# One kernel, its instruction order replaced: local and block-summary attention with an FFN behind it, on one Trainium2 core

## The chip, the cores and the metric

The kernel runs on one core of a Trainium2 chip. A core has five engines with an instruction queue each: TensorE (PE, with PEld for its weight loads), VectorE (DVE), ScalarE (ACT), GpSimd (POOL) and SyncE (SP). In this kernel SP does nothing but issue DMA transfers. Engines run their own queues in order and wait for one another by semaphores. The time is the device time of one execution in microseconds (us); the number that counts is the median of several executions.

## The reference: what is computed

The inputs are q, k and v, 4 batches, 8 heads, 768 positions, 64 elements, and the weights of a layer-norm (LN) and of an FFN.

```python
k_sum = k.reshape(B, H, nb, 32, D).max(axis=3)      # 24 blocks of 32 keys
v_sum = v.reshape(B, H, nb, 32, D).mean(axis=3)
mask_l = np.abs(pos[:, None] - pos[None, :]) < 16   # local window
scores_s = scale * einsum('bhsd,bhnd->bhsn', q, k_sum) + np.log(32)
a = softmax(concat([where(mask_l, scale * q @ k.T, -1e9), scores_s]))
x = (a @ concat([v, v_sum])).transpose(0, 2, 1, 3).reshape(B, S, 512)
xn = (x - mu) / sqrt(var + 1e-6) * g_ln
out = x + maximum(xn @ w_ch1, 0) @ w_ch2            # 512 -> 2048 -> 512
```

## The kernel before

The 3072 rows of x (4 x 768) are worked on in 24 tiles of 128 rows. For a tile, the queries of one head meet only a band of keys around them and the 24 block maxima, so the scores are narrow. Tiles 0 to 5, the first batch ("early", in two halves of four heads each, t = 0 to 11: `early_k`, `early_qk`, `softmax`, `early_transp`, `early_pv`) are worked on in float32 while the FFN weights are fetched and prepared. Tiles 6 to 23 ("late": `load_q`, `load_k`, `load_v`, `heads`, `late_softmax`, `values`, `late_out`) are worked on in split float16: a value is carried as a float16 and a rest, and products are summed from several matmuls. Weights arrive as `raw` (512 KB transfers) and are merged to `m` on DVE (`merge_w`); `gram` multiplies them with themselves, the `scales` for each group of rows come from the gram sums, a diagonal matrix `diag` from the scales, and PE then makes `low`, the scaled low-order part of the weights (`split_w`).

The FFN takes two tiles at a time, a group. The step `norm` runs LN over a tile: mean and variance (`mv`) on DVE, the root `rs` on POOL, x16 on DVE, and a DMA transposition of x16 (128x8x128, half a group) to `xt`. FFN stages `g1(s)` make hidden blocks h0, h1, ... (48 or fewer matmuls `h<-xt,w_u` of 256 columns); `g2` and, from group 3 on, `g2_wide` multiply them with the second weights, in banks a or acc_a, acc_s, acc_o; `parts_of` splits the hidden values with tiles called wide, on ACT and DVE. The sums come back as `uv`, are added to x on POOL (`x<-x,uv`) and on DVE, and go out. `batch` makes for each batch block maxima and sums (`kmax`, `vsum`), from loads into `bst`, of which there is one buffer.

What sets the order: none of these operations is issued where its line stands. Class `Plan` records every call of an engine as an entry of `self.ops` (a `unit` joins several matmuls into one), and `issue` (line 159) then issues the entries in the sequence that the constant `ORDER` gives, a compressed list of numbers at lines 58 on. Hence every instruction has line L159 in the trace. The one list orders all five engines: an engine runs its own entries in the sequence that they have in the list, and waits are added where an entry needs another engine's result or a buffer that is not free. DMA issues share 8 semaphores in turn, so that a ninth transfer waits for the first to have landed. Pools, tile sizes and the number of buffers are set by the constants ahead of `ORDER`. `warm` stands for 36 matmuls of the identity matrix `ident` with itself, whose result is not used; `gain` spreads the LN weights over 128 partitions by a matmul with ones.

Of the kernel before, what the change touches and what calls it, by code (L numbers as in the profile page):

```python
# [55 lines left out]
AT = {4: 16, 5: 19, 6: 23, 7: 24, 8: 26, 9: 30, 10: 33, 11: 37, 12: 41, 13: 46, 14: 51, 15: 54, 16: 60, 17: 63, 18: 67, 19: 71, 20: 76, 21: 79, 22: 84, 23: 87}  # L56

ORDER = (
    "c-l3X2Y6Lg_QltE^pKcPrPlxnEkG!t8#*H3U;zcB7You92WCbEDFcEaDxfG*1Qk#;G-*mzno92wK@y~w(BYjuzx(|EKR#Ywx%ZsC*Is+=b#7_hu`5<p"
    "2d#uMtccFreaod{x^LO}Kg_-9E9s2gwrnb???bi2ABARyuh~_b7#bbEWS(DgtERH-G=J||luGG_l~X~jXO%0~NDu71ov{wA+t%&$mn@`n<`n$P!Ifsc"  # L60
    "oKr|<9o^7yy2Wy5buF?a#j1?<SrzTEIGwVh%B}kDM_)yMvUe37u*<ww(>$xD8cMTuHb6yn)^4yub+_C%(qC5DZSm!_jq6G&Ne^wG<xq@1Cze_|N!+XL"
    "8GemXqRXpC$#1n)aL#U7KCl=XdOuu3tL!<|Cbqp+ScSD+kJx;Bp2+uGqApvUyX`xKUJMsecTKjZ-C5r!wAOF*GnM5Ih3o4ZV!L6<nq*CN+V)#_K4rS1"
    "ey$By4V&#MSTy&{unBIV@8%9!5i1kQ^85W*n@vX5+!bG2kGM0w3W%3bs@rWxe03$c4gQ=B4(0I^c|949bNhVj(86$Yx6_*Fpf5x8Np69!<Z@VcS5vv&"
    "bz;dN^4GOc&F!3=J!V_nLm#%BnrmH^&Fx{`g;vES+a7xXY<GjuCI6^?v)bCKJXXj3>f3-%4PwY?$*!0^qNN&Pzk}K%T>ogKo~zlnl-+Q7{c2E}tEcU{"
    "Tj3j6dm>t@RLfF9R}6H<`gJm{-(e|w=yN!)K7O_xp_*;r!`tpHf5yscrEBg#=iY~Qikjqbm0`_FqHmz8cFZ=qRx0ZcsFEF%sM<*%@3w(+Mf+HH6>Gh0"
    "u9~>JzAEeHajX1D8}IU3KD(x5nDh(##8{$hV(Z)~?|63|tXqN7Qr%M#PcEwMa$BnX>{k0GuCgzoOq;28Zn3@YkHE=6Hb(DRF`cmSYN#f*MY-YZ9gEg4"
    "+G>qe+D<4<Md1H(z2h(1eivi8Ky#-(R1RC|T9eHk7}?0SDTUp}_-U%>;^?_5TH%kAM=6&|&7RV?*4Ul3tE%K5(^rc11(f3ExG%Z#Ghdiq`q5>x4K~u="
    "RWq%#*7{!2)>2<;lAoZ~s!d;hrCvnxhh3rmZ`uQ!%5L%6XwQUpg!jPf7!|S|%5N7~znO~LS$^B(JGi#i&~~bUt#a*rrlxD0KcPgsuCIJAozf*+qA7ld"
    "3aNr+!tY0@?|y&C)mI(6VBKML61s9lk5id+ze{ndVjE$>9XNAY$E*_T4AiUcWxI}we5nsXJzW>z=3Q!*XkWNQy0W76WyN}S&WaO3H~DZ_IZ=#;egil*"
    ")sO0o9>nP?j2!Mp``?s|qCB+Ez1e(M!rItA?b3F8)!x%%>h0IL!*p}-`%L!=pNdk4WZMi*e`<`LQxq#Zed_vi|8`YYVVmS?=`*XPH~e%r%ujS9{CXE<"  # L70
    "jcuAsq?WN(8b!JZORHNU+p4B?RwKU?ZL4DwU9wsc(OT8hUK{G)bxEvO3-0}@>x#EBusCE7)S6Z6npdiy>Ka-d6!N0W@?WX3{y>wrTLa7HirZ=JvUaFm"
    "NmTWaE}}^BI%==mx2Us$cwJ>jC(l|_vT3GUK9}p~deg(>U0OIz^%Zo-F-x&DrP$;8mA^Gmumb4vHmip+#-V~4uqsObaEroSLx=n?KDT>RE#3FwuI^)B"
    ")1B}sZk_ef9A5{7cldTL%@=h~(Qj$tMAtx@?Kmo4z&^HXzByM^baTS}-8a6n3szm_3pwxmx|t|QJ$Ks<`s{8bTHrLwP4J2Ch=0Ldw=}<)ie6Cx>e3>#"
    "k)1QOF&wrQp%?smwX|h)#~gLHb}mMfL9UI<w8cI(RLZ{aO+!U(i8XaU`I|OS?^;jx%%S4$jG=hUf=W6}o{gPpbGWMZs+rpy26dMnK5M2TI%1ufI8k)W"
    "d3ADI!qv4xc|l`axKXI0ZT9KJz17cmlYBmxKZwJ%x5D<kJKzrxZAxfoxU%xQ2ihLKppNcNcpu*$P<7Tj=lc3Bii2ZMxi!88x>+amjepvOG|lS!Xcw<p"
    "=;6OD3yxK=bQQFVaCN2HE0=SAsh+fTYU`%c4W-b(T*?HiG-?&2Emnr_2dk(5PIc4~C3;;QwAa^gWw~~<vdP;4e+=#<X%l_k))u%fO!&^srCatncmAN="
    "zOEanPprOGceCtwKL~ElclGThy#S|v^GR;L&9M&dHF`6f*6WZTtkP~S)2O?4syAIaQ4=)Ey7;lG<UH4;pzQCdp*4iP+tfAC8#mM{Fk{NNN^0x#tB0=H"
    "vuMXmTY$!7*fLwF|Ej!oL8s%H;*Pod9CP&x`f8bdp}?O6ZlN|D@1XB&lHF05X;lkUCuoa;&QC*O9@ugH!{V9TLFVt+Kb2Fr6l3G<6HP-$@+$%Lzo4SF"
    "UmfubJ?O}bXxxk1uj@WdU9Bcc_`PnT?c1z+#F;EbQL3RD&B69R8f%*^pF3u|tQ+?&w;xcYA!vJ&8*C@-4K>m*o$%$=!%eo~R)^Xx)AJh0T>8>x!N}D("
    "qsOSrli-mUOiexT-LzP3EddpHo)}9~nLN5{ziFy1qTgnNMh`7PZ`<?fo^{b;6t6X}In-0;KSOPz^eK3bv$uKIiaF3qsc7g$`-b`Po^JTjdY^yOEd$M+"  # L80
    "z!ZvA&(QR6YrCteeuk?KGaK6`TwFVlc%Sa+g)^9E{WY8^HwFAo>z*&*s)crk(OG*_GkAT~7SgFX;g-`J`;Ms*72#Xp(Xyykc~uQ93OB$-o@3ILCfkak"
    "W#J5JPzHZ_)2fAf_<z|Y++vnxfaVNp_K{832%JMFT?fn7RPwSC?4}*EuW=(sEO+S3a4aer7b@Ym*mf#4&30S+(9Q5o+i3OB_*&px4&*v$4KpFjhM|`W"
    "a5WcjDTlZsy9R;mO75zo-T2-0?DHdzrz6#CM^s1A+-vs09Sx6HEgKTL7mm^6IKES^pwF~#K=~pQsy_WPM91+db+y#p4^L)BRL8Yt;G_$a@h$rcb?jts"
    "QIjXM+={sr?tK$yTbjGl-SfVqp0kR28Yh}yYlx&gl|5)J^poWZ<%B<dsa){Bt#1)|_pLs}H}11*;P;OGo1V!F@~xSCtGK@#`rl7u=#XC`8WBy`jkK@a"
    "6#pAjxF#_t(vdNAWEGY32VAUz9=mJ>(U1qY=X5+vIh@e~OCY0n^){}n8pzFLHV=m{Neb4z%KBT$X{g#!tCo7wRrgQgQ=92UoY+t;qu-uEm-e~s_}T@o"
    "v459U({Mr8tv|0<tt@_O9@;!b>DCwiZgT_tDD`7%p76bGvg)~mJ_=V=l>HnPPu6Wb;0oTq;>P;6%-P+XGm>CflqwP59(r<=HPaFeu*23{=a?K<bj<JL"
    "yFzZ8UkLhfOvqT)7_HweY-P~e-e5PC{(DL#ao|_z-4lKkeX;`Qw4Lsp%JlwFUsLNP%!ExAa)H0}C}AEtz615F45F8aY9}2VB8~vbCOF~w_Jpg7S6OR;"
    "E3HMP-lrQcz~?CSf{#~WU0*8m66c&KT+;-bN2m9<ajr1;{)|ctv}av&8)!dK%??cXhSVq6r(VQoZ?O6<6P^7p3_NRTR?rP$>Sj|3YIzX-OvAUo$Fx39"
    "r3$)di6j>;=qM5V!b}LN-c~=*M}wJmXE>qlM#C0pmaVZ(c+3J^7gX^UZgGaDfXJI@!2r529X5=`pOZISn?`1*L1h+f?1$Fhp&G~0&aJ4&96D}2r=8w#"
    "Fu3!yUekD=%6|Pck+?_V7yE&7UG=x8$)OsPco=oL4LU1q75W~-OgU_waI`aQrJkVscU#~JejxUHRDUX!Oa{Np)|am9OT5SM-MPWFIcJiyOp-%>Jcz8Z"  # L90
    "z088mc7yd>(UpN`nrSQTbM<AP54h(T_(Tgw!yZ9hC&0u{RgG+>Yd%wQ2j{<Za=A^8eNc%paA7`KwxNzC(7=wc>0#hG=--ZTd^J;M4qmn@=yxQpd(856"
    "^zQ5UtvT>&Fn&FsO5@Nwa(8=tzz9w|$I<UN?p{ls7e~~6DiMF6Hh71%c*`^PPus)pv($$Z+bT{Rb-7{{Q+FLK&!L~G<9*aG6($uV?w(}23S4`j#hdI;"
    ">w$W`jb5FEv3pVZMRZCdI6DIbdN6^4{0pObi{WfM>$HT)|6(eS<nH2}d+IWaAEk1=IqSWT>P-RTaZIJ!WHkb%7!6BCvCi*QXcP*3*80Gs85+&5CG|2f"
    "*3(3y9ti@&nWx#9Oz|4exxJkYQd>?_(JHPkoJ~upJQM8`@>xzVOh>b$abOATSdDqN!XH&T^t%Xm&cL;HVC{wAe+ykb4EA|p$K#sn6Wj@AP*dIaFY8&>"
    "?*}4Z*ej7I8^@{Ua8?<@6-{tbWl`1Acz{Ltliv6r@p~ur*LbR&gu{4)S^Npz+K&h}vExcxi#m;hxen%}!q`-hd&ws0B`Pux7A-*2b5q|QRA)9Pgf5(?"
    ")}W&!nUF<5>=lqPCe+*N$#icDwo5osC(~I|*)g4dTTA|qj0U3~Df%9bZ_aP|(Vk3ez-e<6{V)h+2qJ8RFY@rF2Dp3xudm`9=E9*v<QJkwl{Jo-mlMxI"
    "ChS78xQ_zu1HDG5Yj%a)AR7%QvuqkCx^eX0Jot7AcT*Qfo`Bo=1g#BLtHJkqsqKF7?xuYD3tu#dy-G06qZK^siAJHy!mh4dS(^WORDs<%wbFwr>I|n-"
    "R1>Y4&NU@L|0rD&kL#_jCtz2yD#P%xxY*edOea`8`V~XW2Vwdm6k;#&Hc~9>eWrQjxCQ_5G4)@GdL_Ba%+6171kb^pMj$=_H$0u$u@z2az<`6yxWk-H"
    "Cc)xjU|tO5_mj!X>>N1D1l^C|zKa}wM~nVNCv`(50_{sA!!amP6?QwW7PbKf&w$+*S+g7+_>lfdpf_rv3umZDPX&%68+WaNaW5!%!u2bi^%`y}l^kx{"
    "WNXg14K+m1QoY^wD)VlUUbDdUeqg~I|4^^;%copBnCfN2gWQfhHw&ipVH{NgYQGA^OOsD3-<-!y90%#XsPSMj53bE1<Ce^f@?_K*#V*E)axW7r3Op+k"  # L100
    "Yh85bwtY<v>*5(s;S>(qI}u-8i4N(8m--Kr`T*U$gjsmn4&Zz~0?|bJIe6|@0Y&?WX;J|sN3-f%U^ya!UKSJlF1(osezBZLiqPc)B7OV@HM?$sZl7X}"
    "gH|Ns^5bA^OB{E3c+`YnD&fQ`z`QlQCMkHbcn6iQ2iAcvD6gXMF9W<c)0<cLCh(p4U`?7mNyh}JbSKAnlxGn$sw%5@)=M^1fo~s9Hx1Da3!XpK;ADOe"
    "9gd;rojTC($>e^J&jEfV;d?BV&7^~(nIKgaJYPH#na3URyXA=DMfzw1x;GItcTwTBRQL>2aU}Q0!L%$YwVN37@hQ-%jWG8nceG|c^dhfd?gUR>b5Rcm"
    "hWp{b{m7H0(@d8WDE<Sk_`x3Hmf8^6ACY;RP8W}d@#Q0PupCO!9aULGM@~Z{c2b9pRG|sIKTM_2=a<1UA6{<)I((Df>ID1mL^x6`g5P;+nn`Xatq?gU"
    "pn6B?%UqG3h>FbjJ8-U;f^*4jbikn&e}aEb-fgEw1tT>I>i+k$-MkUDW>bDvx{KoHQ~|IGa>>beS0if#D_^t!e+`~I=ZV}KLxdp(d!)m$Vv)~*+8&KO"
    "p^j$fLQIAzRg64IE*iNflSy@hDIQ#Vm*3t0{rfxi4DS5<bCAz@IOovIum#Vcy#*)M;IDzO@hLmM{tpwyAg="
# [996 lines left out]
```

## Time and profile before

| what | us |
|---|---|
| median of 3 executions | 596.71 |
| lowest, highest | 595.60, 597.96 |
| the profiled execution | 598.19 |
| its span, first to last instruction | 596.4 |
| busy: PE, PEld | 576.2, 466.1 |
| busy: DVE, ACT, POOL | 488.9, 413.9, 128.8 |

The profiled execution is one of its own, 1.5 us above the median. A row of the trace is one instruction or several equal ones in a row; in brackets it has the idle time of its engine ahead of it, and what ended it. Matmuls are pipelined: a row's length is the sum as modelled, and equal ones overlap.

### The profile page before, as it was taken

To read this page: it belongs to the slowest core of one execution; us is meant where nothing else is said; L and a number is where in the kernel's file an instruction comes from. 1 tells how busy PE (TensorE), PEld (TensorE's weight loads), DVE (VectorE), ACT (ScalarE), POOL (GpSimd) and SP (SyncE) were. 2 spreads that over 40 slices of the span, in tenths; PEclk is the share of its full clock that TensorE was granted. 3 is DMA by queue.
4 is the path that set the end of the run, shared out by engine and by line. 5 is a ranking of instruction groups with operands and counts; after the bars stand their busy time and mean duration, and the time that the engine had idled before them with its cause. 6 is when DMAs were issued, how large, how long until landed. Compare 5 with 4: busy or idle time off the path is not lost.

```text
span 596.4 us, 16606 instructions
## 1 busy us (share of the span) xinstructions
PE 576.2 (97%) x6440; PEld 466.1 (78%) x6440; DVE 488.9 (82%) x1290; ACT 413.9 (69%) x1043; POOL 128.8 (22%) x213
## 2 busy tenths in 40 slices
...
GB/s 286 242 276 282 257 253 245 224 98 114 129 156 118 138 156 123 148 95 147 163 124 121 129 65 109 93 108 118 81 118 94 89 70 75 81 71 41 36 2 35
DMA packets 108484, 79.19 MB, mean 133 GB/s; under 512 B 68733, under 2 KB 94973, under 8 KB 108406
## 3 DMA queue, kind: packets, MB, share of 16 engines
...
## 4 chain that ended last, share of the span: by engine, by line
PE 41%; DVE 12%; ACT 6%; DMA 4%; issue 3%; SPq 1%; POOL 0%; ACTq 0%; DVEq 0%; POOLq 0%
PE h L159 20%; PE acc_a L159 8%; PE acc_s L159 6%; PE acc_o L159 5%; DVE h_x L159 3%; DVE wide L159 3%; DMA bst<-in_ks 2%; ACT p L159 2%; ACT h_x L159 2%; PE o L159 1%; DVE x L159 1%; SPq L159 1%; PE s L159 1%; DVE p L159 1%; ACT wide L159 1%
## 5 line engine op out<-in xcount | busy, mean ns | idle before, releaser
L159 PE MATMUL h<-xt,w_u 128*128 128x256 f16 x2304 | 265.7, 273 | 3.5 <-DMA xt<-x 1.1
L159 PEld LDWEIGHTS <-w_u 128*128 128x128 f16 x2304 | 224.1, 98 | 34.6 <-issue 6.6
L159 PEld LDWEIGHTS <-h_x 128*128 128x128 f16 x1752 | 170.7, 98 | 45.5 <-issue 0.6
L159 DVE TENSOR_TENSOR h_x<-wide,h_x 128x896 f16<-128x896 f32 x72 | 80.6, 1128 | 23.5 <-ACT h_x L159 23.0
L159 ACT CAST h_x<-wide 128x896 f16<-128x896 f32 x72 | 66.5, 934 | 47.1 <-DVE wide L159 46.9
L159 DVE TENSOR_TENSOR wide<-wide 128x128 f32<-128x128 f32 (+1 forms) x224 | 78.8, 363 | 19.8 <-ACT wide L159 17.5
L159 POOL TENSOR_TENSOR p<-p,p 128x480 f16<-128x480 f32 x36 | 43.7, 1219 | 136.9 <-ACT p L159 107.1
L159 ACT ACTIVATE wide<-h 128x512 f32<-128x512 f32 x72 | 41.8, 590 | 40.9 <-DVE h_x L159 22.1
L159 ACT ACTIVATE p<-p,mn,sv 128x120 f32<-128x120 f32 x144 | 68.5, 477 | 1.2
L159 PE MATMUL acc_o<-w,h_x 128*128 128x256 f16 x408 | 55.8, 273 | 0.0
L159 PE MATMUL a<-w,h_x 128*128 128x512 f16 x240 | 53.0, 379 | 0.0
L159 POOL TENSOR_TENSOR x<-x,uv 128x512 f32<-128x512 f32 x18 | 24.4, 1362 | 127.7 <-DVE uv L159 108.7
L159 ACT ACTIVATE bst<-bst 128x384 f32<-128x384 f32 (+2 forms) x55 | 32.3, 586 | 23.7 <-DVE vsum L159 15.0
L159 PE MATMUL acc_a<-mix_x,h_x 128*128 128x256 f16 x324 | 45.5, 273 | 0.0
L159 PE MATMUL acc_s<-mix_x,h_x 128*128 128x256 f16 x324 | 43.9, 273 | 0.0
L159 DVE SCALAR_TENSOR_TENSOR m<-raw,m 128x512 uint32<-128x512 uint32 x64 | 43.0, 684 | 0.4
L159 DVE CUSTOM_DVE_ANT_0 p<-s,mask 128x120 f32<-128x120 f32 x144 | 36.9, 274 | 7.6 <-POOL p L159 7.6
L159 POOL TENSOR_SCALAR rs<-mv 128x1 f32<-128x1 f32 x24 | 12.8, 534 | 112.0 <-DVE mv L159 103.8
L159 PE MATMUL acc_a<-w,h_x 128*128 128x256 f16 x216 | 35.5, 273 | 0.1
L159 ACT ACTIVATE v<-vst,sv 128x512 f16<-128x512 f32 x36 | 25.4, 712 | 4.9 <-DMA vst<-in_va 3.3
L159 DVE SCALAR_TENSOR_TENSOR v<-vst,sv,v 128x512 f16<-128x512 f32 x36 | 27.5, 767 | 1.2 <-ACT v L159 1.2
L159 ACT ACTIVATION_READ_ACCUMULATOR p<-p,mn,sv 128x1 f32 x144 | 27.0, 188 | 0.0
(140 smaller groups left out, 843.8 us busy)
## 6 DMA issues: line engine op xcount, KB each, us to landing
...
```

What stands on the lines that cost most here:

```text
L159: getattr(getattr(nc, engine), op)(*a, **k)
```

## The change

Only the constant `ORDER` is replaced. The recorded entries, hence all instructions, shapes and buffers, are those of before; the sequence is another one. It was searched on a model of the core in which each GpSimd operation that reads SBUF takes its turn at the port that it shares with VectorE.

```diff
 ORDER = (
-    "c-l3X2Y6Lg_QltE^pKcPrPlxnEkG!t8#*H3U;zcB7You92WCbEDFcEaDxfG*1Qk#;G-*mzno92wK@y~w(BYj
...
+    "c-l3X2Yl33_QlT|AQVFifrKtfkOb*1bRjeWX-n_8uplCfs|dEWAd0|
...
 )
```

(Both lines are cut.) The macro sequence of tiles, weight parts and FFN stages is as before. Inside it most entries move by a few places. Three places follow; the names have the buffer numbers of the program, `_83` and the like.

PE's first rows before. gain is the spread LN weights, s0 the scores of tile 0, whose stationary matrix (spare_x6) is built from keys and block maxima, while spare_x0 are queries.

```order
L159 MATMUL gain_98<-xn1_97,ones1_70 128x512
L159 MATMUL warm_96<-ident_67 128x128 x36
L159 MATMUL s0_0_101<-ident_67 128x128
L159 MATMUL s0_0_101<-spare_x6_93,spare_x0_86 64x128 x2
L159 MATMUL s0_1_102<-spare_x6_93,spare_x0_86 64x128 x2
```

After, the two first rows have changed places. SP's first rows are, before and then after:

```order
L159 DMA spare_x9_83<-in_ks 128x768
L159 DMA xn1_97<-in_g_ln 1x512
L159 DMA spare_x11_85<-in_ks 128x768
L159 DMA spare_x8_82<-in_ks 128x768
L159 DMA blk_79<-in_blocks 128x144
L159 DMA spare_x10_84<-in_ks 128x768
L159 DMA raw1_0_225<-in_w1 128x4x256
L159 DMA spare_x1_89<-in_va 128x2x256 x2
L159 DMA spare_x0_86<-in_qe 128x512
L159 DMA vend_92<-in_vb 32x2x256
```

```order
L159 DMA spare_x0_86<-in_qe 128x512
L159 DMA xn1_97<-in_g_ln 1x512
L159 DMA spare_x8_82<-in_ks 128x768
L159 DMA spare_x9_83<-in_ks 128x768
L159 DMA spare_x11_85<-in_ks 128x768
L159 DMA spare_x10_84<-in_ks 128x768
L159 DMA blk_79<-in_blocks 128x144
L159 DMA spare_x1_89<-in_va 128x2x256 x2
L159 DMA raw1_0_225<-in_w1 128x4x256
L159 DMA spare_x3_90<-in_va 128x2x256
```

The first queries (in_qe) have moved from the tenth transfer to the first, the four key loads stand together, and the first weight transfer (raw1_0) stands behind the values.

DVE, where the scales of the third quarter of the first weights are made from gram1_8 (about 57 us into the trace); bst12 is a load of keys, kmax1 their block maxima, m1_12 and m1_14 merged weights. Before, and then after:

```order
L159 TENSOR_REDUCE scales_72<-gram1_8_276 128x1
L159 SCALAR_TENSOR_TENSOR h0_y0_356<-h1_359,h0_y0_356 128x512
L159 TENSOR_REDUCE kmax1_369<-bst12_378 128x12
L159 TENSOR_SCALAR scales_72<-gram1_8_276 128x1
L159 TENSOR_SCALAR scales_72<-scales_72 128x1 x2
L159 TENSOR_SCALAR m1_14_254<-raw1_15_255 128x512
L159 SCALAR_TENSOR_TENSOR m1_14_254<-raw1_15_255,m1_14_254 128x512
L159 TENSOR_SCALAR rc8_198<-sum8_194 128x4
L159 SCALAR_TENSOR_TENSOR m1_14_254<-raw1_15_255,m1_14_254 128x512
L159 TENSOR_SCALAR diag2_277<-ident_67,scales_72 128x128
```

```order
L159 TENSOR_REDUCE scales_72<-gram1_8_276 128x1
L159 TENSOR_SCALAR m1_12_250<-raw1_12_249 128x512
L159 TENSOR_SCALAR m1_14_254<-raw1_15_255 128x512
L159 TENSOR_SCALAR scales_72<-gram1_8_276 128x1
L159 TENSOR_SCALAR scales_72<-scales_72 128x1
L159 SCALAR_TENSOR_TENSOR m1_14_254<-raw1_15_255,m1_14_254 128x512
L159 TENSOR_SCALAR scales_72<-scales_72 128x1
L159 TENSOR_SCALAR diag2_277<-ident_67,scales_72 128x128
```

The reduction of bst12 and one of the steps of m1_14 now stand behind diag2, and a step of m1_12 stands ahead of it.

SP at the third group of FFN rows (xt_3, about 192 to 200 us into the trace); bst53 to bst56 are loads for block sums, x16_6 and x16_7 the normalised rows of tiles 6 and 7, the two halves of the group. Before, and then after:

```order
L159 DMA_TRANSPOSE xt_3_473<-x16_6_472 128x8x128
L159 DMA bst54_530<-in_vs 96x512
L159 DMA out_x<-x2_154 128x512
L159 DMA bst55_531<-in_vs 96x512
L159 DMA vst0_68<-in_va 96x256
L159 DMA_TRANSPOSE xt_3_473<-x16_7_491 128x8x128
L159 DMA_TRANSPOSE pt0_345<-p16_344 128x8x128
```

```order
L159 DMA bst53_529<-in_vs 96x512
L159 DMA bst54_530<-in_vs 96x512
L159 DMA kst11_567<-in_kt 64x2x368
L159 DMA_TRANSPOSE xt_3_473<-x16_7_491 128x8x128
L159 DMA bst55_531<-in_vs 96x512
L159 DMA_TRANSPOSE xt_3_473<-x16_6_472 128x8x128
L159 DMA bst56_532<-in_vs 96x512
```

The two halves have changed places, and between them stands one load, bst55. On PE the first reader of xt_3, h24, stood behind six matmuls of 512 columns (a2_1 with h22's values) that now stand between h24 and h25. Other places that the text below speaks of: the values of tile 2 (`vst0_68<-in_va`, early) are issued three rows earlier on SP; PE's first reads of xt for h64 have more matmuls between them and the transposition than before, those for h81 fewer; and acc_a's first products of the third wide stage come later on PE.

## Rows read from the trace of the kernel before

**Rows 1.** The page: busy time of PE, share of the span, instructions.

```profile
PE 576.2 (97%) x6440; PEld 466.1 (78%) x6440; DVE 488.9 (82%) x1290; ACT 413.9 (69%) x1043; POOL 128.8 (22%) x213
```

**Rows 2.** Waits of PE: what for, us in total, times, longest.

```profile
PE gain L159 <- DMA xn<-in_g_ln: 4.2, 1, 4.2
PE low L159 <- DVE diag L159: 1.3, 1, 1.3
...
PE acc_a L159 <- DVE x L159: 0.6, 1, 0.6
...
PE s L159 <- DVE mn L159: 0.3, 1, 0.3
```

**Rows 3.** Busy time by stretch; last: granted clock, DMA share, GB/s.

```profile
0.00:15.00 15.00, 9.88 (x57) 7.78 (x58) 7.12 (x15) 2.58 (x6) 8.48 (x43) 1.00 0.88 286
15.00:60.00 45.00, 42.72 (x454) 28.08 (x453) 38.99 (x155) 42.09 (x151) 10.23 (x40) 1.00 0.93 267
...
140.00:215.00 75.00, 74.13 (x712) 41.68 (x711) 72.27 (x169) 55.22 (x141) 16.52 (x16) 1.00 0.53 134
```

**Rows 4.** Timeline of the head: start, length, engine, operation, idle before it.

```profile
1.20 0.29 POOL masks.py:199 TENSOR_SCALAR_AFFINE_SELECT ident<-ident 128x128 f32<-128x128 f32 x1
...
4.19 2.04 PE L159 MATMUL gain<-xn,ones 1*128 1x512 f32 x2 [4.19 <-DMA xn<-in_g_ln]
...
5.53 0.48 SPq L159 DMA_DIRECT2D spare_x<-in_qe  x1
...
6.16 6.61 PE L159 MATMUL warm<-ident 128*128 128x128 f32 x36
...
9.73 0.94 DVE L159 TENSOR_REDUCE kmax<-spare_x 128x24 f32<-128x768 f32 x1
...
13.81 0.67 PE L159 MATMUL s<-spare_x,spare_x 64*64 64x128 f32 x16 [0.93 <-DMA spare_x<-in_qe]
```

**Rows 5.** Timeline: the values of tile 2, their issue and their use.

```profile
31.91 0.67 SPq L159 DMA_DIRECT2D vst<-in_va  x1
...
37.84 0.27 PE L159 MATMUL o<-vst,pT 128*64 128x64 f32 x1 [1.01 <-DMA vst<-in_va]
```

**Rows 6.** Timeline of DVE from the gram sums to diag2.

```profile
57.44 0.29 DVE L159 TENSOR_REDUCE scales<-gram 128x1 f32<-128x128 f32 x1
...
59.88 0.55 DVE L159 TENSOR_REDUCE kmax<-bst 128x12 f32<-128x384 f32 x1 [1.55 <-DMA bst<-in_ks]
...
61.24 0.69 DVE L159 SCALAR_TENSOR_TENSOR m<-raw,m 128x512 uint32<-128x512 uint32 x1
...
62.58 0.28 DVE L159 TENSOR_SCALAR diag<-ident,scales 128x128 f32<-128x128 f32 x1
```

**Rows 7.** Timeline at h64: SP's two transpositions and PE's first reads.

```profile
415.60 2.65 SPq L159 DMA_TRANSPOSE xt<-x  x2
...
420.47 1.80 PE L159 MATMUL h<-xt,w_u 128*128 128x256 f16 x15 [1.13 <-DMA xt<-x]
```

**Rows 8.** Timeline of SP, PE and PEld up to h24, whose matmuls follow.

```profile
193.85 0.67 SPq L159 DMA_DIRECT2D bst<-in_vs  x1
...
195.78 7.29 PE L159 MATMUL a<-w,h_x 128*128 128x512 f16 x33
...
198.32 0.31 SPq L159 DMA_DIRECT2D bst<-in_vs  x1
...
199.20 1.24 SPq L159 DMA_TRANSPOSE xt<-x  x1
...
202.72 5.30 PEld L159 LDWEIGHTS <-w_u 128*128 128x128 f16 x48 [0.15 <-DMA xt<-x]
```

**Rows 9.** Timeline of DVE, POOL and PE at one collision at the port.

```profile
516.61 1.78 DVE L159 TENSOR_TENSOR wide<-wide 128x128 f32<-128x128 f32 x3
516.78 1.26 POOL L159 TENSOR_TENSOR x<-x,uv 128x512 f32<-128x512 f32 x1 [10.43 <-DVE uv L159]
...
521.47 0.95 PE L159 MATMUL o<-v,pt 128*64 128x64 f16 x48 [0.56 <-ACT wide L159]
```

More of the change, by code (lines that the diff above doesn't have):

```diff
@@ L58 @@
 ORDER = (
[L59 to L106, printed above, removed]
+    "c-l3X2Yl33_QlT|AQVFifrKtfkOb*1bRjeWX-n_8uplCfs|dEWAd0|>i>Oo!iZlfw(p%^~AVh(H^j@S3Y4h%WC;!i%&xg#+Z(h0Y-gC}9Zz}4(-Lk6s"
@@ new lines @@
+    "-Ac(Upe(y)1yn|tc^{{n7R$RFi&K<d4@?ZM2-FMaSYh3^$!@9t-O4Faecd|0*`icKN34SGSdvy)(5mQ~HPTA+)<nGm3xZcI*UBrOiYsW#>~NrKu!1hw"
+    "V|r-MX_Y;pYC34k?L8f{)0Snmb=q3%7b_#DfSS0VJ@9Ako;7wy{cqOGE%$xgW}l!djGStt*||3VZ`p18)w-%_U`Oztg{!)|?RQuwDQ{MPcgUAfZJn|^"
+    "R-ILMTZ9U;|3!OT-2!ui<;g*!Yv-O14pc32F^^0ntE_&o-sE7BP0|9Z;3`=tGY|C8Z?IMhcbUGr&MMiB2=;V!EtR#$sJl&c@n*K)V%#y6@sTdp)e0_D"
+    "lJ?tNdsPQjKq6Q7$mB|*9;~x=--^0|3i|49n?Glr$>Zak@RAL5hkb;;v_UGT6icz!T>-nvr(14T(5b(RahbL|n4p3#-IvoLOLpJ;K`zJVchPQZuqH9("
+    "62}7juP(al!Lm9>eZFS*s_L$#oaBhr&^#h2uC>JH{Sm7d$PVsMBbBifg{h7%`PKF|ady@jrTg}}q!<_B%iB*nuQ03Wyk%InZ%1vtt+8slZWmPE>S>u;"
@@ new lines @@
+    "xkx`>2^Qz}TU!_B|FZdtRVO>H>NZ1_!A5D<-ri?s9p+YJ&OAMDdq6<8`rCE8Vzb?NvJp@zZL=0y<!bvQ8fY)-ANHGawcV1u)01HHxSW$^`ogZTs~Zfs"
+    "HMZOJ_1E>tr*o?9*4jPc=c%EJxRn-e`FOX}`r8~e(FVm>yrrwTj#>gy?6e%!^QSc0wkb=6t)Lt3b8VvScQgDq78Yplw`!|3pbCXuBcDx-5jvtLK<aid"
+    "m1K`t>rY?YHORx&R5f7qYnEpF)XiFw`3g42wXraE*>7F!22AnF$Nwa|V9Uw+N{#m)=oRYH+lK3P`$%nB_p0jJ3GMJLbW7Fzarc5>tTR43(As+&?fO|W"
+    "E3M&b!z%l=-i9dFKGqlTWQq^yo-*tu*VVUGG$&l|YVqAGHc_MfpDN{p?uIqAV|-InpX+D+;Jdp~{*IdPq`BMbJGppY#Wk{1I;6&S)_&A~{Vu8)tH*4)"
+    ">+JXIH$O~8G|Ub4_tn&Ppa@s2rKPy-_5$Z?LfjSYC|Dmz^^1f2>vmO@tg`J<Wj!KG4ed|8qZ$4tmDsC>Hs6J6Q_xPjAwE_4-4E8!&vW1T%`V%wvh6Mk"
@@ new lines @@
+    "R1bACeTHtTh5y=J2)?Bc+%%t~Zu-XO2gh-mt`XE>m=9Wh?N=kX-$aA`KJ8PYvVD8|5?;(^^Z+-`s+-d({b_Zn(KFWDy<|`6u#WTeA*#~Of8@roYB%?z"
+    "pW@!|o0QHPZTxO@?4C+k4Kki&sV>(#k&D`S``u7}wPaoe&YNF*tq|4Q!^z{+*B{btbf%-7SHP;eL-r&Y@M`XNk~^m@YR361DA#tQmX&O?n)3dVHLzu9"
+    "a!p&O&UOO^tpPX3R8i+Gq_Vj-!#XJ5VmRMZRQV^B*AvR};ck;X1Jb)#=fLIQ+thED7HPH>h1s>Ni#Edde2P|zTF6<nTZUG@s71a*pot#^voBds@D^=f"
+    "p#Kl7vJ%|_U(`AUz6y49chQx-KFT!)$5(wbcg$CEdwq<mftkl#P3`rOyno!S3MROCw>tPxBlWGXgAzRF)&#Ru$ZETXmf;7YS4)(p$^I7gcZzpseWspu"
+    "ab$9VZyp%r2U=fuU8Svrru!U=cl)fQb#T#|k0NaIjRUE{!ET0K*YipZwhEjNmIir(<IUU_Uw}+hcHvs?n-EvCz|~-~o8_NzrYg44S43eO1y1-xm=%wz"
@@ new lines @@
+    "?IMQ9RFr;KRVS=|AT5}v-MR{T(t=smIIz?=v7PEo{+&KRTOL`Win*VyEB&aIowS>3<G!%kteF`MciVkU#kr0CE>DBOR7KcbwNyTr6HL)%y{uWjtQM-i"
+    "V*N1pp+@>Pt|MAG2rk6hFwJ7MSo@m=*tMHQFyf!;V}sC{YE){wrRt#n)}8mi=xw`0e|Xn6gQR8lrdFdDAs#-9?r))rjcfwywi^ze@|j?+G+nlty#QX8"
+    "qfP(Rbd+wrg((h}_M-0%(-@!N^6BrIOWzp4`rECv{oq<zf3nim8alJ*=@~!U3XMY>@~gXFOnm>QnmfUEw0p~DTN~>~PyZdng*0ggy8S)fGa0@-uNtWO"
+    "Kzzq&4bl6SrgOe4``)8>45c$vbr-FJO|VY%+6iR4k{R0B+{S_To~+hR@j3~EYP(mgq@DxMPNk{RKuw{itkX>Is7bDRp`Bf<yH5I<x~@{zM~f`rrr66c"
+    "Cc#y+_u=_ny3A+xCG$VFNVm}Xq8s@%ncjSZZhx4Vn#12ojJ*XDlU342>I<-QOiR4icwWcg1eUVrL%j@J+7t09oXY~;^c&QddUkMAt%uFA)r@`@H<KUT"
```

27 lines of the change are left out of this document (added).

## The prediction, made before the result was known

> **What bounds the kernel now.** I read the page first: TensorE (PE) is busy for 97% of the span [rows 1], so only the rest, and work that PE would do later or earlier for the order of the others, can be won by a permutation. The second view is PE's waits, summed by what ended them [rows 2]: 17 lines, from 4.2 us down to 0.3 us, 15.8 us together. One of them, the first, is longer than 1.4 us, so the change has to win at many small places or at the start. The third is busy time by stretch [rows 3]: for the first 60 us the 16 DMA engines are 88 and 93% busy, and VectorE (DVE) is busy 72.27 of the 75 us from 140 on, so there it has 2.7 us to spare.
>
> The granted clock is full in all these stretches [rows 3], so nothing is to be won there. The operations are the same ones before and after, so no term below is for work added or removed; every term is a wait.
>
> **The head.** Today PE's first instruction is the row-broadcast of the LN gain, and it waits 4.19 us for a DMA; then come its 2.04 us, 36 warm-up matmuls (6.61 us), and 0.93 us of waiting for the first queries, so that the first scores start at 13.81 [rows 4]. In the new order the warm-up stands first, and waits for the identity matrix alone, which GpSimd ends at 1.20 + 0.29 = 1.49. So: 1.5 + 0.1 for the hand-over, + 6.6 + 2.0 + 0.3 for the identity matmul = 10.5, that is 3.3 us earlier. The data must be there: the queries, issued tenth at 5.53 today, are now issued first; the four key loads are followed by their maxima, the last of which runs at 9.73 today [rows 4], and is the last to be waited for then too. With one 0.94 us reduction, a small copy on GpSimd and one on ScalarE behind it that leaves the scores at 10.9 to 11.3: 2.9 to 2.5 us won. The other end is 0: the DMA engines are nearly full until 60 us [rows 3], and a PE that is 2.5 us ahead meets transfers that are not. I take -2.5, near the upper end, because in the 45 us from 15 on PE stood still for 45 - 42.7 = 2.3 us at most [rows 3], and of these only 1.01 us at a transfer [rows 5].
>
> **The two waits of the early stage.** (a) PE waits 1.01 us for the values of tile 2, which were issued at 31.91 and were first usable at 37.84, some 5.9 us later, on full engines [rows 5]. The issue moves three rows up on SyncE's queue (SP), past one load of queries and two others; rows of such a queue are 0.4 to 0.7 us apart, so -1.2 at best. But PE comes 2.5 us earlier if the head is right: 0 at worst. I take -0.5. (b) PE waits 1.31 us for the diagonal matrix diag2 [rows 2]. DVE has its gram sums at 57.44, then reduces a block-maximum that itself waits 1.55 us for a load, and ends diag2 only 5.4 us after the gram sums began [rows 6]. In the new order this reduction stands behind diag2; between them are now three steps of conversions, none longer than 0.69 us [rows 6], and three short scale steps, none longer than the 0.28 us of diag2 itself. 0.29 + 3 x 0.69 + 4 x 0.28 = 3.5 us at most, against 5.4. The wait goes, -1.3; 0 is kept as an end, for the raw weights of those conversions may be late by as much. What is next behind it, the low-order matmuls, has nothing else to wait for in the trace.
>
> **The transposed rows.** A DMA transposition on SP takes its x16 rows to the layout that the first FFN matmuls read. Its issue to the first use by a waiting PE is 202.72 - 199.20 = 3.5 us, and the same (from the second of the pair that starts at 415.60, so about 416.9) to 420.47 [rows 7, 8]. (a) At h64 PE waits 1.13 us for it [rows 7]. In the new order there are 4.69 us of matmuls between the issue of the transposition and h64, where there were 1.85 (matmuls of 256 columns follow one another every 0.109 us: 15 take 1.80, of which 0.27 is the last one [rows 7]; the list is counted with that): the wait goes, -1.1 (0 to -1.3). (b) At h24 it goes the other way. There 18 matmuls, 1.94 us by the same count, lay between the second transposition of the group and h24, and PE waited 0.15 us [rows 8]. Now none do: six matmuls of 512 columns are put behind the first h24 ones, 6 x 7.29 / 33 = 1.3 us [rows 8], and the transposition of the other half of the rows stands behind a load of bst. PE comes 1.3 us early and finds the rows not there. What it loses lies between 0, if the layer-norm before it is ahead too, and 1.94 + 1.3 + 0.15 = 3.4; the 1.3 us come back as work in hand, which speaks for 1.4 to 2.3. I take +1.8. The Trainium skill, "VectorE: DVE Perf Modes", section "The three transpose paths", gives 1309 ns for one 128x128 block by the DMA's transposer; with that behind the 1.24 us of issue the rows would be there an estimated 2.55 us after the start, 1.0 us sooner than here, and the sum 1.0 lower. Here the transposition is one of eight such blocks, and its 3.5 us decide. (c) At h81 the matmuls between fall from 4.69 to 2.29 us, under 3.5: 3.5 - 2.29 = 1.2 is the most it can lose, and 0 where the issue is earlier than the list's place tells. +0.5.
>
> **The rest: the shared port.** The trace shows the collision: three additions in SBUF on DVE, 128x128 each, take 1.78 us while GpSimd's x<-x,uv runs for 1.26 at the same time, and PE then waits 0.56 us for the result [rows 9]. (Of three such pieces the first was stretched; what follows on it is one wait of about half a microsecond.) The Trainium skill, "SBUF — State Buffer", section "Who interferes with whom", says the same: a VectorE instruction with two SBUF inputs contends with a GpSimd instruction that reads SBUF, and the lock holds for a whole instruction, with whoever came first. Waits of the PE that are left after the head, diag, vst and xt are 15.8 - 4.2 - 0.9 - 1.3 - 1.0 - 1.1 = 7.3 us [rows 2], in pieces under 0.9. They go when the late product comes in time, and others come for them: the GpSimd instructions are as many as before, and only their partners change. At least one piece is seen to be relieved: the read of acc_a, 0.6 us [rows 2], comes some 10 us later in the new list. The places in the list where a product is consumed with less matmul work between than its producer lasts fall from 20 to 13 from 140 us on, a third; a third of 7.3 would be -2.4, all gained pieces at 0.36 us; with as many new ones, +2.5. I take -1.5.
>
> **The sum.** -2.5 - 0.5 - 1.3 - 1.1 + 1.8 + 0.5 - 1.5 = -4.6. Against the profiled execution of before, 598.19 us (its span 596.4 and 1.8 around it), that is 593.6. The median of the three runs of before is 596.71, 1.5 lower, so 592.1.
>
> **The rivals.**
> - Everything goes: head -2.9, vst -1.2, diag -1.5, h64 -1.3, h24 and h81 at 0, the rest -2.6: -9.5, so 587. For it: the order spaces nearly every hand-over wider. Against it: no permutation takes all of 7.3 us of small waits, and h24 has no matmuls in between.
> - The head's gain is given back. PE starts 2.5 us earlier, but up to 60 us the DMA engines are at 93% and ScalarE and DVE at 42.1 and 39.0 of 45 [rows 3]; PE then waits the same 2.5 us in pieces at the first transfers, and vst gives nothing. The port collisions are moved, not fewer (the change doesn't do what it says): the rest is -0.5. 0 - 1.3 - 1.1 + 1.8 + 0.5 - 0.5 = -0.6: 596.
> - Slower. In SP's queue the transposition for h24 now stands behind the load bst55, whose buffer is single and must have been read by DVE. Such loads follow one another at 193.85 and 198.32 in the trace [rows 8], 4.5 us apart, and DVE there has little time to spare. If PE stands at h24 as the first half is issued, it waits for one such cycle, the issue (1.24) and the transfer (3.5): 9.2 us in place of 1.8. With the rest at 0 (DVE, late at one place, is late at the next) the sum is -2.5 - 0.5 - 1.3 - 1.1 + 9.2 + 0.5 = +4.3: 601. It decides from about 7.9 us at h24 on; against it, the first of the two loads may be issued much earlier than today, as its row stands earlier too.
>
> **How the numbers follow.** My forecast, 592.1, has a chance of 0.55; with its terms' bounds it runs from 588 to 595.5, and 0.42 of the 0.55 lies below 593.7. Everything goes: 0.12. Gain given back: 0.21. Slower: 0.12. A measurement of this kernel can tell about 0.5%, 3 us, from no change, so faster is below 593.7 and slower above 599.7. Faster: 0.42 + 0.12 = 0.54. Same: 0.13 + 0.21 = 0.34. Slower: 0.12. The range leaves out the slower case alone: 586.5 to 598.5.
>
> **What the profile after would show.** Head: warm before gain, and the first scores at 10.9 to 11.3; if PE's busy time from 15 to 60 falls under 42 of 45 us, the gain is given back. Diag: no wait of PE for diag at 60 us, and diag2 within 3.5 us of its gram sums. Transpositions: no wait for xt at h64, one of 1.4 to 2.3 at h24 (over 5: the slower case). The port: DVE's busy time some microseconds under its 488.9; if it isn't, the collisions have only moved. The prediction is wrong if the sum of PE's waits does not fall from 15.8 to about 11, or if it falls and the span doesn't.

## The result, and the profile after

The new order takes 590.29 us (median of 4 executions, 589.16 to 591.44) where the old one took 597.34 (4 executions, 595.60 to 598.00). The ratio is 0.989, with an interval of 0.986 to 0.992: 7.0 us faster, outside what a measurement of this kernel can mistake for no change. Ratios, here and below, are estimated from the executions that were not in the core's slower state, and can differ by 0.1 to 0.2% from the quotient of the medians. The forecast was 592.1, 4.6 us less than 596.71. The profiled execution took 590.32 us with a span of 588.3.

The page after, the row that answers to [rows 1]:

```profile
PE 574.5 (98%) x6440; PEld 464.7 (79%) x6440; DVE 487.1 (83%) x1290; ACT 412.7 (70%) x1043; POOL 126.7 (22%) x213
```

DVE and POOL are busy for 1.8 and 2.1 us less than before; if less contention at the port shows anywhere on this page, it is no more than that. PE's waits after, to be held against [rows 2] (what for, us in total, times, longest):

```profile
PE s L159 <- POOL spare_x L159: 2.4, 1, 2.4
PE warm L159 <- POOL ident masks.py:199: 1.5, 1, 1.5
PE o L159 <- DMA pt<-p: 1.3, 1, 1.3
PE h L159 <- DMA xt<-x: 1.0, 2, 0.6
PE h L159 <- DVE h_x L159: 0.9, 1, 0.9
PE s L159 <- DMA spare_x<-in_qe: 0.7, 1, 0.7
```

Twelve lines, 9.7 us, in place of 17 with 15.8. The line for diag is gone, and so are those in which PE waited for DVE's v, x, ql and mn; two new ones stand at the head (`POOL spare_x` and `POOL ident`), and one behind it (`pt`). Where the time went is plainer in the busy time by stretch. One stretch of 121 us, before and then after (the columns are those of rows 3):

```profile
215.00:336.00 121.00, 117.96 (x1474) 104.69 (x1474) 100.93 (x274) 91.54 (x218) 29.35 (x33) 1.00 0.56 138
```

```profile
215.00:336.00 121.00, 121.00 (x1550) 107.67 (x1549) 105.39 (x290) 96.08 (x235) 25.52 (x30) 1.00 0.54 134
```

PE stands still for 3.0 us of it before, and not at all after; it starts 1550 matmuls there in place of 1474. (A row counts a matmul as busy to its modelled end, so the true gap is likely larger than 3.0.) Set out by equal amounts of matmul work, PE after is level with PE before at 30 to 60 us, 2 to 3 us ahead from 75 to 195, 6.3 ahead at 270, 7.7 at 315, and 8.0 at the end. The head, on which I had set most, gives nothing:

```profile
1.55 6.17 PE L159 MATMUL warm<-ident 128*128 128x128 f32 x36 [1.55 <-POOL ident masks.py:199]
7.65 1.12 PE L159 MATMUL gain<-xn,ones 1*128 1x512 f32 x2
8.70 0.33 PE L159 MATMUL s<-ident 128*128 128x128 f32 x1
11.43 0.67 PE L159 MATMUL s<-spare_x,spare_x 64*64 64x128 f32 x16 [2.40 <-POOL spare_x L159]
12.03 3.27 PE L159 MATMUL v<-spare_x,blk 128*120 128x512 f32 x4
15.08 0.42 PE L159 MATMUL s<-ident 128*128 128x128 f32 x1
...
24.40 0.78 PE L159 MATMUL s<-spare_x,spare_x 64*64 64x128 f32 x16 [0.72 <-DMA spare_x<-in_qe]
...
44.99 1.27 PE L159 MATMUL h<-xt,w_u 128*128 128x256 f16 x10 [0.63 <-DMA xt<-x]
```

The first scores stand at 11.43 where they stood at 13.81 [rows 4]. At the identity matmul behind the four `v<-spare_x,blk` the lead has shrunk from 2.4 to 1.1 us, since these four take 3.27 us; before they took 1.98. By h1 nothing of it is left. The two rows before that answer:

```profile
14.41 1.98 PE L159 MATMUL v<-spare_x,blk 128*120 128x512 f32 x4
...
44.38 1.47 PE L159 MATMUL h<-xt,w_u 128*128 128x256 f16 x12
```

### The profile page after: what moved, and what is told of

Read it like the earlier page. It is cut to its first block, busy times and chain, and to the rows that moved or that the text cites. A ratio compares the mean times of both kernels' runs of the same rounds, so it can differ in the third digit from the quotient of the medians.

```text
span 588.3 us, 16617 instructions
## 1 busy us (share of the span) xinstructions
PE 574.5 (98%) x6440; PEld 464.7 (79%) x6440; DVE 487.1 (83%) x1290; ACT 412.7 (70%) x1043; POOL 126.7 (22%) x213
## 4 chain that ended last, share of the span: by engine, by line
PE 70%; DVE 12%; DMA 8%; ACT 4%; issue 2%; SPq 1%; POOL 1%; ACTq 0%; DVEq 0%; POOLq 0%
PE h L159 31%; PE a L159 10%; PE acc_a L159 9%; PE acc_s L159 6%; PE acc_o L159 6%; PE o L159 2%; PE low L159 2%; DVE h_x L159 2%; PE s L159 2%; DVE x L159 2%; DMA xt<-x 2%; DVE wide L159 2%; DMA spare_x<-in_qe 1%; DVE p L159 1%; DMA spare_x<-in_va 1%
## 5 line engine op out<-in xcount | busy, mean ns | idle before, releaser
L159 PE MATMUL h<-xt,w_u 128*128 128x256 f16 x2304 | 263.9, 273 | 2.1 <-DMA xt<-x 1.0
L159 PEld LDWEIGHTS <-w_u 128*128 128x128 f16 x2304 | 223.7, 98 | 32.0 <-issue 1.8
L159 PEld LDWEIGHTS <-h_x 128*128 128x128 f16 x1752 | 170.7, 98 | 44.7 <-issue 0.3
L159 DVE TENSOR_TENSOR h_x<-wide,h_x 128x896 f16<-128x896 f32 x72 | 82.1, 1145 | 16.9 <-ACT h_x L159 16.5
L159 DVE TENSOR_TENSOR wide<-wide 128x128 f32<-128x128 f32 (+1 forms) x224 | 79.7, 361 | 19.5 <-ACT wide L159 16.9
L159 ACT CAST h_x<-wide 128x896 f16<-128x896 f32 x72 | 66.9, 932 | 40.2 <-DVE wide L159 40.0
L159 POOL TENSOR_TENSOR p<-p,p 128x480 f16<-128x480 f32 x36 | 43.1, 1201 | 193.1 <-ACT p L159 153.7
L159 ACT ACTIVATE wide<-h 128x512 f32<-128x512 f32 x72 | 42.4, 592 | 52.8 <-DVE h_x L159 29.8
L159 ACT ACTIVATE p<-p,mn,sv 128x120 f32<-128x120 f32 x144 | 68.5, 477 | 1.2
L159 PE MATMUL acc_o<-w,h_x 128*128 128x256 f16 x408 | 55.8, 273 | 0.0
L159 PE MATMUL a<-w,h_x 128*128 128x512 f16 x240 | 53.3, 379 | 0.0
L159 ACT ACTIVATE bst<-bst 128x384 f32<-128x384 f32 (+2 forms) x55 | 32.2, 586 | 20.2 <-DVE vsum L159 11.9
L159 POOL TENSOR_TENSOR x<-x,uv 128x512 f32<-128x512 f32 x18 | 25.0, 1400 | 96.2 <-DVE uv L159 96.0
L159 PE MATMUL acc_a<-mix_x,h_x 128*128 128x256 f16 x324 | 45.2, 273 | 0.0
L159 DVE CUSTOM_DVE_ANT_0 p<-s,mask 128x120 f32<-128x120 f32 x144 | 36.0, 273 | 10.1 <-POOL p L159 6.7
L159 PE MATMUL acc_s<-mix_x,h_x 128*128 128x256 f16 x324 | 43.9, 273 | 0.0
L159 DVE SCALAR_TENSOR_TENSOR m<-raw,m 128x512 uint32<-128x512 uint32 x64 | 42.9, 683 | 0.4
L159 PE MATMUL acc_a<-w,h_x 128*128 128x256 f16 x216 | 35.4, 273 | 0.0
L159 POOL TENSOR_SCALAR rs<-mv 128x1 f32<-128x1 f32 x24 | 13.5, 563 | 95.9 <-DVE mv L159 90.1
L159 ACT ACTIVATION_READ_ACCUMULATOR p<-p,mn,sv 128x1 f32 x144 | 27.0, 188 | 0.0
L159 ACT ACTIVATE v<-vst,sv 128x512 f16<-128x512 f32 x36 | 25.4, 713 | 1.7 <-DMA vst<-in_vb 0.8
L159 DVE SCALAR_TENSOR_TENSOR v<-vst,sv,v 128x512 f16<-128x512 f32 x36 | 26.4, 743 | 0.0
```

Source lines behind the costliest of these rows:

```text
L159: getattr(getattr(nc, engine), op)(*a, **k)
```

## The experiments

Each kernel is the one before or after with another `ORDER`, or with one edit. A spliced list takes the first n entries of one list, then those of the other that are still missing, in their order there. The lines of `ORDER` are fewer in these kernels, so the trace has L157 where it had L159. Theories: that stalls are local and what a stretch wins is kept; that the head is the source; and that the shared port is what the new order avoids, against hand-overs that merely stood too near in the list.

### Which stretch of the list brings the gain

```diff
-order = before
+e1_head    = after up to h1, then before
+e2_rest    = before up to h1, then after
+e3_second  = before up to h1, after up to h22, then before
+e4_third   = before up to h22, after up to h48, then before
```

> The order of after up to its first FFN matmul (h1, 45 us in the trace of after), the order of before for all that is not issued by then. Theory G (the head's lead is given back: between the traces PE is 3.9 us ahead at 12.6 us, 2.0 ahead at 15 and level at 30 to 45): the time of before within 0.7 us. Rival H (my prediction's term; the lead is kept): -2 to -2.5 us.

> The order of before up to its first FFN matmul (h1, 44 us), the order of after for the rest: the mirror of e1_head. Theory G: nearly all of the gain, -6.5 to -7.5 us against before. Rival H: the gain without the head, -4.5 to -5.

> The order of before, but between the first matmuls of h1 and of h22 (44 to 154 us) that of after. Theory K (stalls are local, and what one stretch wins is kept to the end): PE's stalls of this stretch fall from about 5.7 to 3.2 us between the traces (diag 1.5 of it), so -2 to -2.5 us. Rival L (DVE, 95% busy there, sets the pace of the next stretch, so a lead of PE is given back): 0 to -0.7.

> The order of before, but between the first matmuls of h22 and of h48 (154 to 336 us) that of after. Theory K: PE's stalls of this stretch fall from 5.3 to 0.2 us between the traces, so -4.5 to -5 us, the larger part of the whole gain. Rival L: these stalls go only because the stretches ahead ran otherwise, so -2 or less.

All four ran on one chip, against 599.22 us of before.

| kernel | us, median | ratio to before, interval |
|---|---|---|
| e1_head | 600.68 | 1.002 (0.999 to 1.004) |
| e2_rest | 591.73 | 0.988 (0.985 to 0.990) |
| e3_second | 599.48 | 0.999 (0.996 to 1.002) |
| e4_third | 590.88 | 0.986 (0.983 to 0.989) |

The head's order brings nothing, or costs a little; the rest alone brings the whole gain. In e3 the stretch from 44 to 154 us brings nothing either that this can tell (its interval reaches from -2.5 to +1.0 us). The stretch from 154 to 336 us alone brings 8.3 us (6.5 to 9.9 by the interval), more than the 5 that its stalls had promised and all that the whole change brings. Each kernel has one trace, of one execution, and executions of the same kernel differ by several us: the traces here are of executions of 604.18 us (e1, its slowest), 591.65 (e2), 599.53 (e3) and 588.51 (e4, its fastest). The row from 215 to 336 us, for e4 and then for e3, whose list there is that of before:

```profile
215.00:336.00 121.00, 121.00 (x1549) 107.56 (x1547) 103.39 (x284) 93.19 (x227) 26.55 (x30) 1.00 0.53 131
```

```profile
215.00:336.00 121.00, 115.38 (x1449) 102.17 (x1448) 98.88 (x268) 89.14 (x215) 28.93 (x33) 1.00 0.56 133
```

In every trace with the new list from 154 to 336 (after, e2, e4, and e6 and e11 below) PE is busy for 121.00 of these 121 us, in e12 for 120.91; with the old list, for 115.4 to 118.0. What e3's PE had won by 154 us (its busy time from 45 to 154 is 107.25 of 109, against 105.59 before) it loses again here: its h22 starts at 151.9 us, where e1, e5, e9 and e10, which have the list of before from h1 on (but for the single moves of e9 and e10, below), start theirs at 153.3 to 154.5, and its h48 at 333.1, theirs at 332.2 to 333.4. That is what rival L says; that DVE's pace is the reason isn't shown by it.

### Is it the shared port?

```diff
-tensor_tensor(lo, p, hi, ALU.subtract)
+tensor_tensor(lo[:, :, :1], p[:, :, :1], hi[:, :, :1], ALU.subtract)
-tensor_tensor(x0[:], x0[:], uv[:, :2]..., ALU.add)
+tensor_tensor(x0[:, :1], x0[:, :1], uv[:, 0, :1], ALU.add)
-tensor_tensor(x1h, x1h, twice(w, 0), ALU.add)
+tensor_tensor(x1[:, :1], x1[:, :1], w[:, :1], ALU.add)
```

> The order of before, but GpSimd's two long readers of SBUF, p<-p,p (36 of 1.2 us) and x<-x,uv (18 of 1.36 us), work on one column per head or row instead of all: the low parts of the probabilities and the part of the sum in uv are left out for the other columns, and everything waits for them as before. Theory P (the collisions at the port make the late stalls of before): the stalls beyond 154 us, 8.6 us in the trace of before, fall by 4 us or more, and the time by 4 to 6. Theory T (hand-overs that stand too near in the list, and collisions only add a little): -0.5 to -1.5.

> The same cut of GpSimd's readers in the order of after. Theory P: the order of after has already taken the collisions' cost, so 0 to -1 against after (-7 to -8 against before). Theory T: as much as in e5_thin_before, -0.5 to -1.5 against after. If the port cost both orders the same, e5 and e6 lose the same amount, 2 us or more.

With the old list the thin readers gave 596.07 against 599.57, ratio 0.995 (0.992 to 0.998); with the new list 588.00, ratio 0.982 (0.979 to 0.985), where after itself stands at 0.989 on another chip and at 0.987 on a third (e12). So each list gains some 3 to 4 us, and the intervals do not tell the two apart. By the medians that is more than theory T had said, and equal losses of 2 us or more were the case in which the port costs both orders the same. The costliest DVE group that collides, before, after and in the two thin kernels (busy time and mean ns of one stand behind the bar):

```profile
L159 DVE TENSOR_TENSOR wide<-wide 128x128 f32<-128x128 f32 (+1 forms) x224 | 78.8, 363 | 19.8 <-ACT wide L159 17.5
```

```profile
L159 DVE TENSOR_TENSOR wide<-wide 128x128 f32<-128x128 f32 (+1 forms) x224 | 79.7, 361 | 19.5 <-ACT wide L159 16.9
```

```profile
L157 DVE TENSOR_TENSOR wide<-wide 128x128 f32<-128x128 f32 (+1 forms) x224 | 72.8, 335 | 25.0 <-ACT wide L157 22.7
```

```profile
L157 DVE TENSOR_TENSOR wide<-wide 128x128 f32<-128x128 f32 (+1 forms) x224 | 73.6, 334 | 25.9 <-ACT wide L157 23.1
```

The mean of 363 ns is 361 with the new list and 335 without GpSimd's long readers: collisions slow these steps as much in the new list as in the old. And without the long readers the old list's stalls stay. The stretch of e5 and then of e6:

```profile
215.00:336.00 121.00, 116.26 (x1486) 102.66 (x1475) 96.78 (x272) 90.51 (x220) 15.21 (x33) 1.00 0.57 136
```

```profile
215.00:336.00 121.00, 121.00 (x1550) 107.65 (x1548) 102.49 (x290) 95.51 (x233) 10.97 (x29) 1.00 0.56 135
```

Theory P falls: with GpSimd's busy time in this stretch halved, PE still stands still for 4.7 us with the old list. The stalls are made by the order of the steps, not by the port. (The trace of e5 is of an execution of 599.04 us, 3.0 above its median; the reading rests on its stalls being there at all, with e6 beside it, and not on their size.) The port costs both lists about the same. (The thin operations are also shorter for those who wait for them, so the 3 to 4 us are not the port's price alone.)

### The stretch in two halves

```diff
+e7_third_a = before up to h22, after up to h29, then before
+e8_third_b = before up to h29, after up to h48, then before
```

> The order of before, but between the first matmuls of h22 and of h29 (154 to 220 us) that of after: the first half of what gave 8.3 us in e4_third. By the stalls in the trace of before (1.7 of 6.2 us lie in this part): -1.5 to -2.5. By the view that DVE, busy 59 of 61 us here, is what runs late into the next stretch: -4 or more, since the ones behind go with it.

> The order of before, but between the first matmuls of h29 and of h48 (220 to 336 us) that of after: the second half. By the stalls (4.5 of 6.2 us lie here): -4 to -5. By the view that DVE comes late out of the stretch before: -2 or less, and the stalls move.

e7 gave 597.23 and e8 596.25 against 599.57: ratios 0.997 (0.994 to 1.000) and 0.994 (0.992 to 0.997), that is -1.9 as the stalls said for the first, and -3.3, a little less, for the second. Together they make 5 us, the sum of the stalls; both at once, in e4, 8.3. The other 3 us may be the chip's difference (the intervals are 3 us wide), or the halves help each other. A part of them is in the yardstick. The 5 us were read from one trace, and the execution in it stood still less than others with the old list here: from 154 to 336 us PE is idle for 3.9 us of 182 in the trace of before, for 5.3 to 6.1 in e1, e5, e9 and e10, and for 0.4 or less in after, e2, e4, e6, e11 and e12. Against those four the new list is worth 5 to 6 us here. And the trace of e4 can't give the size: its execution is 4.3 us ahead of before at h22 (149.7 against 154.0), up to which the two lists are the same. In e7 PE is busy for all of the 61 us from 154 to 215, and then stalls from 215 on (116.71 of 121) as the other traces with the old list there do. Its h48 starts at 330.9 us, 1.3 us or more ahead of e1, e5, e9 and e10, but no earlier than in before (330.7); by the median some 2 us are kept.

### Single moves inside that stretch

One stall of [rows 2]'s kind could be followed to its source. PE's h47 takes a PSUM bank that DVE frees when it makes x13 from o13; x13 takes the buffer of x7; and x7's transfer to the output stands only 20 places ahead in the list. The rows before:

```profile
308.83 0.95 PE L159 MATMUL o<-v,pt 128*64 128x64 f16 x48
...
310.09 0.42 SPq L159 DMA_DIRECT2D out_x<-x  x1
...
313.91 0.69 DVE L159 TENSOR_TENSOR x<-o,lrc 128x512 f32<-128x512 f32 x1 [1.31 <-PE acc_o L159]
...
314.65 0.60 PE L159 MATMUL h<-xt,w_u 128*128 128x256 f16 x4 [0.84 <-DVE x L159]
```

The profile puts DVE's 1.31 us down to PE's acc_o, but o13's matmuls had ended at 309.78 (308.83 + 0.95); what came last for this instruction is the transfer issued at 310.09, which the profile's chain of work that ended last has landing 3.70 us later, at 313.79. In the new list that transfer is issued at 269.44, 40 us earlier.

```diff
+e9_out7: the list of before; out_x<-x7 moved from place 1780 to right behind x7's last sum
+e10_out7_kmax: e9, and kmax3<-bst73, kmax3<-bst74 (each with its square on ScalarE)
+               moved behind ql12 and behind h31's parts
```

> The order of before with one entry moved: the transfer of x7 to the output, 20 places ahead of x13<-o13 (which takes x7's buffer) in the list of before, goes right behind the last sum of x7, 183 places earlier; in the order of after it stands 184 places ahead. Theory Q (a transfer late in SP's queue blocks DVE at x13, and PE's h47 behind it): the stall of 1.0 to 2.0 us at h47, some 314 us into the trace, goes: -1 to -2 us. Rival (DVE would have been late anyway): 0 to -0.5.

> e9_out7, and two block maxima of the next batch (kmax3 of bst73 and bst74, for whose loads DVE stands still 1.48 and 1.84 us in the trace of before) moved behind the steps that PE waits for: kl, ql and h31's parts. Theory Q: the stalls at 244 to 246 us (1.3 us) go too, so 1 to 1.5 us more than e9_out7. Rival (DVE's backlog of this stretch, not its waits): the same as e9_out7 within 0.5, and the stalls stay.

Measured on one chip with e11 and e12, against 600.45: e9 599.16, ratio 0.999 (0.996 to 1.002), and e10 600.26, ratio 0.998 (0.994 to 1.001). The stall itself went. The same rows in e9:

```profile
315.07 0.68 DVE L157 TENSOR_TENSOR x<-o,lrc 128x512 f32<-128x512 f32 x1
...
315.54 0.82 PE L157 MATMUL acc_o<-w,h_x 128*128 128x256 f16 x6
316.20 2.02 PE L157 MATMUL h<-xt,w_u 128*128 128x256 f16 x17
```

x13 follows its predecessor with no gap, and h47 follows acc_o. So the chain is shown; that its 1 to 2 us are kept to the end is not, since the total moved by less than the interval, which holds -1 and 0 alike. e10 did not work: the wait of 0.62 us for ql at 246 went, but PE then waited 0.59 us for pt ahead of it and 0.58 for xt behind it, and the stretch's busy time is 116.23 of 121, no better than before. Two late loads were not the cause of that stall, or not alone: my theory Q holds for the stall at h47 and falls for 244 to 246.

### A try at a better version

```diff
 order = after
+the transposition pt1 of tile 17 moved on SP ahead of two vst loads that wait for their buffer
-WARM = 36
+WARM = 54
```

> The order of after, with one transposition of probabilities (pt1, of tile 17) moved on SP's queue ahead of two loads of vst that wait for their buffer, and 54 warm-up matmuls in place of 36. Theory Q: the wait of 1.34 us for pt at 402 goes and is kept: -1.3 against e12_after. Of the warm-up, the granted clock stays at its upper level and the first 512-column matmuls take 0.43 us instead of 0.82, 1.3 us that are given back by 45 us: 0. Rival: the head's 1.3 us are kept too, -2.6 in all.

> The order of after, as it is, on the same chip: -7 us against before, for the comparison with e9 to e11.

e11 took 592.17 us and e12, the new order unchanged, 591.67 (ratios to before 0.987 each, intervals 0.983 to 0.992 and 0.983 to 0.991): no gain. The wait of 1.3 us for pt went in e11, and the one of 0.39 at h81 with it. But in the profiled execution one early transposition came late:

```profile
46.46 0.72 PE L157 MATMUL h<-xt,w_u 128*128 128x256 f16 x5 [2.38 <-DMA xt<-x]
```

That is 1.7 us more than after had at the same place, and e12's trace has no such wait. Whether it takes away in the other executions what the edits won isn't shown: this one took 589.82 us, the shortest of e11's six. The longer warm-up did not keep the clock either (below).

## Why the prediction was right, and where it was not

The number came out within 2.4 us of the change's 7.0, and the direction is right. But three of the seven terms were wrong, and their errors cancelled: that the sum came so near is in good part luck.

- **The head, -2.5: wrong.** The working up to the first scores was right but for 0.1 us (10.9 to 11.3 forecast, 11.43 measured; as forecast, the last key load and its maximum, copied by POOL, ended the wait). The failed step is that it would be kept. I took -2.5 rather than 0 because PE had only 2.3 us of gaps from 15 to 60 us; but a PE that comes earlier makes new gaps at the same data. It met slower matmuls at 12 us and in_qe (0.72), was level by 30, and then met xt of h1 (0.63). The sum took the granted clock as full throughout, and had no term for the first of these. The sign set for a gain given back, PE busy for less than 42 of the 45 us from 15 on, did not show it: it was 42.19, for slower matmuls count as busy. e1_head gives +1.5 us by the medians, 0 by its interval. That is the rival "the head's gain is given back", to which I had given 0.21, true in its first half.
- **The values of tile 2, -0.5, and diag2, -1.3: the mechanism right, the worth not shown.** After, diag2 ends 2.7 us behind the start of its gram sums (59.48 + 0.29 - 57.04), where I had at most 3.5, and neither wait is in the list. But e4 has the list of before here, and its waits have no line for diag at all, while e10 with the same list has 1.3 again. The early stage varies from execution to execution with the landing of its loads, and a single profile cannot price its stalls. e3 says what the stretch with diag is worth in the end: nothing that can be measured.
- **h64, -1.1: right as to the place.** No wait for xt there after. In e9, with the old list, it was still 0.7 us; in e4, with the old list there and the new one ahead of it, 0.4. So the wait in the trace of before, 1.1, was at the upper end.
- **h24, +1.8: wrong, it cost nothing.** The failed step is to take places in the list for time. The list said that no matmul lies between the transposition and h24; but SP runs ahead of PE and is held by its own buffers, and these came free earlier (the load bst55 went out at 194.26, in [rows 8] at 198.32):

```profile
194.69 1.41 SPq L159 DMA_TRANSPOSE xt<-x  x1
...
198.60 2.78 PE L159 MATMUL h<-xt,w_u 128*128 128x256 f16 x24
```

  The transposition is 4.5 us earlier than in [rows 8], h24 4.3 (its first matmul there is at 202.90), so 3.9 us lie between them where 3.7 lay: the 0.15 us of waiting are covered, by little. The slower rival rested on this step and fell with it. (Its 9.2 us also held the 1.24 us of issue twice, since the 3.5 us are counted from the start of the issue; counted once they are 8.0, and that rival's sum +3.1.) The Trainium skill's figure for one 128x128 block ("VectorE: DVE Perf Modes", "The three transpose paths") was not needed, and no run here tests it.
- **h81, +0.5: right.** PE waits 0.39 us for xt there, by the rows after.
- **The rest, -1.5: the sign right, the size not.** This term was sized by a count, a third of 7.3 us of small waits. From 215 to 336 us alone 3.0 us or more went, and e4 shows 8.3 (6.5 to 9.9) for the stretch with the 61 us ahead of it: this was the change. And the reason that I weighed for it, the port, was not the one: by e5 and e6 the old list has the stalls with and without collisions, and the new one in neither case. The Trainium skill's rule ("SBUF — State Buffer", "Who interferes with whom") agrees with the traces as to who slows whom: DVE's wide steps fall from 363 to 335 ns without GpSimd's long readers. But it says nothing of who waits for the slowed ones. Of the collision in [rows 9] the reading went too far: it was the second of the three additions that was stretched (516.81, 1.38 us), and PE's wait of 0.56 us, ended by ACT some 3 us later, was not shown to come from it.

With what the runs show in place of these three terms, they would be: head 0, h24 0, the third stretch -5 or more. What I had listed as evidence, fewer hand-overs with less matmul work between than the producer lasts (20 to 13 places beyond 140 us), pointed the right way, and I marked it down to -1.5 for fear of as many new ones; its -2.4 would still have been half or less.

What stays open: how much of the 3 us between the two halves of the stretch apart (5.2) and together (8.3) is more than noise, and which moves, besides that of x7's transfer, make up the gain. The single moves tried are below what a measurement can tell.
